# Chunked attention ahead of two gated products: from block 2 on two pairs of heads in one step, values and scores in one TensorE block, the first product on two PSUM banks

## Chip, core and metric

The kernel runs on one core of a Trainium2 chip. The metric is the device time of one execution in microseconds (us), the median of several executions.

## The reference

```python
# q, k, v: (4, 8, 768, 64); 8 memory keys and values for each head
for c in range(S // 32):
    l_start, r_end = max(0, 32 * c - 16), min(S, 32 * c + 32 + 8)
    k_full = concat(mem_k, k[:, :, l_start:r_end]); v_full = concat(mem_v, v[:, :, l_start:r_end])
    a = softmax(q[:, :, 32 * c:32 * c + 32] @ k_full.T / 8)      # sum + 1e-9 below the line
    out[:, :, 32 * c:32 * c + 32] = a @ v_full
x = out.transpose(0, 2, 1, 3).reshape(3072, 512)
h = x @ w1_in; x = (h * tanh(softplus(h))) @ w1_out              # 512 -> 2048 -> 512
h = x @ w2_in; return (h * sigmoid(1.702 * h)) @ w2_out          # 512 -> 2048 -> 512
```

The weights come in as 64-bit floats and are converted on the chip from their two 32-bit words.

## The kernel before

The 3072 tokens are 8 blocks of 384 (TB). A block has 8 heads; two heads that share the 128 partitions are a pair (hp, four of them), and 96 queries with a window of 128 keys are a group, four to a block. An *octet* is one pair of heads with all four groups of a block.

The work has four stages: the first product with the attention in between (`forward` and `quads`, 8 blocks x 16 tiles f of 128 outputs), the product of the first layer's output (`across`), the second layer's first product (`first`) and its second (`second`). From block 1 on, an operand of the first product is split into a high and a low part in a reduced 32-bit type, and a tile f is 4 x 3 = 12 matmuls of 384 columns into one PSUM bank (line 1049). Block 0 uses plain 32-bit matmuls and starts while weights are still being converted on VectorE (lines 377 to 394) and split for the later blocks (490 to 495).

The attention of an octet from block 1 on runs so: from block 2 on, q and k come by DMA in pieces of 32 x 32 and are turned by VectorE (lines 630, 634); `oct_scores` puts 16 matmuls into two banks (742); `quad`, for each half of the octet, takes the masked minimum on VectorE (794), the powers with their sums on ScalarE (809) and, after the inverses of the sums, the scaling on VectorE or ScalarE (829, 837); `oct_out` turns the weights on TensorE (938), copies them out (945, 947), multiplies with the values (959) and evicts the result as high and low part (973, 974, 978) into the next block's operands. Octets use the banks s0, s1 and o0, o1 in turn. A tile f goes in turn to two h banks and to o2 and o3, and is copied out by ScalarE or VectorE (1177, 1178), then sent to DRAM.

The order of instructions on every engine is made by a planner, `Plan`. Each operation is put in with a rank (the tile f at which it is due), a price for each engine that can do it, and what it reads and writes. `issue` runs through time: an engine that comes free takes the ready operation of the lowest rank. The resulting order is then issued; nothing changes it on the chip. The scores of an octet of block j have the rank 16 * (j - 1) - 12 + 4 * hp + 0.5, the tile f of block j has 16 * j + f. A buffer's name (`Tag`) has a number of places, and `Shared` puts buffers into parts of another: before the change q and k as loaded lie in one place each (in z0), as turned in one place each (in z1), and the turned weights in two (z3).

Weights of the later products are converted during the first one, in the order of a list (`layer, p`) with one entry for every 7 tiles f; for layer 1 and p below 4 the result stays in the buffers wo4 to wo15, wo0 and wo1.

Of the kernel before, what the change touches and what calls it, by code (L numbers as in the profile page):

```python
# [23 lines left out]
CUT = 6  # L24
STAGGER = 1.5

# [63 lines left out]

class Part:
# [17 lines left out]
class Plan:  # L109
# [4 lines left out]
    RELOAD = 1.4  # L114
    PATIENCE = 1.0
# [4 lines left out]
    def add(self, rank, ways, reads=(), writes=(), updates=(), chain=None, table=None):  # L120
        op = Op()
        op.table = table
        op.rank, op.ways, op.seq = rank, ways, len(self.ops)
# [9 lines left out]
        for b in (*writes, *updates):  # L133
            for o in b.readers:
                wait(o)
            b = b.whole
            if not b.users and b.tag is not None:
                made = b.tag.made
                k = made.index(b)
                if k >= b.tag.bufs:  # L140
                    b.gate += [(o, True) for o in made[k - b.tag.bufs].users]
                    made[k - b.tag.bufs].closed = True
                if k:
                    b.gate.append((made[k - 1].users[0], False))
# [25 lines left out]
    def issue(self):  # L170
# [14 lines left out]
        while left:  # L185
# [5 lines left out]
            for e in engines:  # L191
# [44 lines left out]
                lag = self.LAG.get(e, 0.0)  # L236
                if size:
# [27 lines left out]
def bus(nbytes, run):  # L265
    return nbytes / 270e3 * (1 if run >= 512 else 1.5 if run >= 256 else 2.5)
# [3 lines left out]
def kernel(  # L270
# [46 lines left out]
    def tags(pool, **bufs):  # L317
# [4 lines left out]
        z0=1, z1=1, z2=1, z3=1, vt=2, e=2, mx=3, sm=3, r=3, mask=1,  # L322
# [410 lines left out]
    def oct_scores(pair, rank, names):  # L733

        s = [T[n].new([GQ, GB, P], F32) for n in names]

        def scores():
            for queries, keys, _ in pair:
                for i in range(2):
                    for hh in range(2):  # L740
                        d = slice(hh * D, (hh + 1) * D)
                        nc.tensor.matmul(  # L742
                            out=s[hh][:, keys(d, i, True), :], lhsT=queries(d, i), rhs=keys(d, i), start=True, stop=True
                        )

        add(rank + 0.5, [("pe", 1.4, scores)], reads=list(dict.fromkeys(pair[0][2] + pair[1][2])), writes=s)
        return s
# [12 lines left out]
    def quad(j, hp, gp, heads, rank, given=None, both=None):  # L760
# [8 lines left out]
        e = T["ev" if j == 0 and hp % 2 else "e"].new([GQ, 2, 2, P], F32)  # L769
# [35 lines left out]
        for hh in range(2):  # L805
            add(rank + 0.6, [("dve", 0.42, lambda hh=hh: least(hh))], reads=[s[hh], mask], writes=[e, mx])
# [11 lines left out]
        for i in range(2):  # L818
            for hh in range(2):
                add(  # L820
                    rank + 1, [("act", 0.6, lambda i=i, hh=hh: power(i, hh))],
# [106 lines left out]
    def oct_out(j, hp, vt, rank, names, es):  # L928

        aTs = []  # L930
        for n, e in enumerate(es):
            t = T[names[n]].new([P, 2, 2, GQ], F32)
            aT = T["aT"].new([P, 2, 2, GQ], F32)

            def turn(t=t, e=e):
                for i in range(2):
                    for hh in range(2):
                        nc.tensor.transpose(t[:, i, hh, :], e[:, i, hh, :], ident[:GQ, :GQ])

            r = rank + STAGGER * n  # L940
            add(r + 2.2, [("pe", 0.33, turn)], reads=[e, ident], writes=[t])
            add(
                r + 2.4,
                [
                    ("act", act(TB, True), lambda t=t, aT=aT: nc.scalar.activation(
                        out=aT.get(), in_=t.get(), func=AF.Copy)),
                    ("dve", dve(TB), lambda t=t, aT=aT: nc.vector.tensor_copy(out=aT.get(), in_=t.get())),
                ],
                reads=[t], writes=[aT],
            )  # L950
            aTs.append(aT)
        o = T[names[1]].new([P, GB, GQ], F32)
        h = 2 * hp if j < EARLY else 2 * hp % HV
        per = GB // len(vt)

        def values():
            for g in range(GB):
                for hh in range(2):
                    nc.tensor.matmul(  # L959
                        out=o[hh * D:(hh + 1) * D, g], lhsT=vt[g // per][:, g % per, h + hh], rhs=aTs[g // 2][:, g % 2, hh],  # L960
                        start=True, stop=True,
                    )

        add(r + 2.7, [("pe", 1.0, values)], reads=[*vt, *aTs], writes=[o])
        if j not in x0:
            x0[j] = Inputs("xh", j), Inputs("xl", j)
        xh, xl = x0[j]
        part = fixed()
        flat = lambda: o.get().rearrange("p g t -> p (g t)")
        add(  # L970
            r + 2.9,
            [
                ("act", act(TB, True), lambda: nc.scalar.activation(out=xh.at(hp), in_=flat(), func=AF.Copy)),
                ("dve", dve(TB), lambda: nc.vector.tensor_copy(out=xh.at(hp), in_=flat())),
            ],
            reads=[o], writes=[xh.buf(hp), part],
        )
        add(r + 3.1, [("dve", dve(TB), lambda: nc.vector.tensor_tensor(
            out=xl.at(hp), in0=flat(), in1=xh.at(hp), op=ALU.subtract))], reads=[o, part], writes=[xl.buf(hp)])

    def quads():

        last = None
        for j in range(NB):
            b, s0 = divmod(j * TB, S)
# [3 lines left out]
            for n in range(NQ):  # L989
# [6 lines left out]
                else:  # L996
                    hp, gp = divmod(n, GB // 2)
                    if gp == 0:
# [5 lines left out]
                        else:  # L1004
                            pair = pair_of_heads(j, hp, rank)
# [544 lines left out]
```

## Time and profile before

| | us |
|---|---|
| median of 3 runs | 1124.51 (1123.49 to 1124.64) |
| profiled execution | 1122.46 |
| its span, first to last instruction | 1120.70 |
| busy: TensorE (PE) | 1103.0 (98%) |
| busy: VectorE (DVE) | 846.5 (76%) |
| busy: ScalarE (ACT) | 604.4 (54%) |

The profiled execution's own time holds what lies around the span. Matmuls are pipelined, so that a busy PE says that no matmul was missing, not that it ran at its peak. PEld is the weight load, which lies beside the matmuls. SP issues the DMAs.

### The profile page before, as it was taken

To read this page: it belongs to the slowest core of one execution; us is meant where nothing else is said; L and a number is where in the kernel's file an instruction comes from. 1 tells how busy PE (TensorE), PEld (TensorE's weight loads), DVE (VectorE), ACT (ScalarE), POOL (GpSimd) and SP (SyncE) were. 2 spreads that over 40 slices of the span, in tenths; PEclk is the share of its full clock that TensorE was granted. 3 is DMA by queue.
4 is the path that set the end of the run, shared out by engine and by line. 5 is a ranking of instruction groups with operands and counts; after the bars stand their busy time and mean duration, and the time that the engine had idled before them with its cause. 6 is when DMAs were issued, how large, how long until landed. Compare 5 with 4: busy or idle time off the path is not lost.

```text
span 1120.7 us, 22456 instructions
## 1 busy us (share of the span) xinstructions
PE 1103.0 (98%) x8226; PEld 1060.7 (95%) x8226; DVE 846.5 (76%) x1865; ACT 604.4 (54%) x1401; POOL 14.7 (1%) x35
## 2 busy tenths in 40 slices
PE   7899999999999999999999999999999999999998
PEld 6567999999999999999999999999999999999998
DVE  5899777987677578898888965747466786877875
ACT  4876555756466456645655565646565543333332
POOL 2000000000000000000000000000000000000000
PEclk9999999999999999999999999999999999999999
DMA  9975878768877946635742676867687735445351
GB/s 171 286 205 129 217 227 232 198 168 223 234 219 247 306 154 214 223 122 174 235 135 76 209 244 221 293 230 248 225 276 245 216 105 155 128 116 157 104 158 50
DMA packets 298222, 217.95 MB, mean 194 GB/s; under 512 B 136120, under 2 KB 276423, under 8 KB 298111
## 3 DMA queue, kind: packets, MB, share of 16 engines
q1 hardware_dynamic: 297759, 215.76, 65.3%
q8 instruction: 65, 1.06, 0.4%
q0 software_dynamic: 352, 0.75, 0.4%
q14 instruction: 46, 0.38, 0.1%
HBM read 135.18 MB, written 81.26 MB: 193 GB/s over the span
## 4 chain that ended last, share of the span: by engine, by line
PE 94%; DMA 2%; SPq 1%; DVE 1%; ACT 1%; issue 0%; DVEq 0%; ACTq 0%
PE h L1049 13%; PE o L1049 13%; PE o L1400 9%; PE o L1308 9%; PE h L1207 9%; PE o L1207 7%; PE h L1400 6%; PE s L1308 6%; PE h L1308 6%; PE s L1400 6%; PE s L1207 4%; PE o L742 1%; SPq L336 1%; PE s L742 1%; PE o L959 1%; PE s L959 1%
## 5 line engine op out<-in xcount | busy, mean ns | idle before, releaser
L809 ACT ACTIVATE e<-e,mx 96x128 f32<-96x128 f32 x240 | 93.0, 392 | 7.3 <-DVE mx L794 7.2
L1049 PE MATMUL o<-xh,wi 128*128 128x384 f32 x320 | 83.6, 342 | 0.0
L1049 PE MATMUL h<-xh,wi 128*128 128x384 f32 x320 | 83.2, 340 | 0.0
L1049 PEld LDWEIGHTS o<-xh,wi 128*128 128x128 f32 x320 | 56.7, 188 | 1.5
L1049 PEld LDWEIGHTS h<-xh,wi 128*128 128x128 f32 x320 | 57.0, 188 | 1.1
L1049 PE MATMUL h<-xl,wi 128*128 128x384 f32 x160 | 53.8, 336 | 0.0
L1049 PE MATMUL o<-xl,wi 128*128 128x384 f32 x160 | 53.7, 336 | 0.0
L1177 ACT ACTIVATE e<-h 128x384 f32<-128x384 f32 (+2 forms) x48 | 22.8, 475 | 45.6 <-PE h L1400 29.6
L809 ACT ACTIVATION_READ_ACCUMULATOR e<-e,mx 96x1 f32 x240 | 45.8, 191 | 0.0
L794 DVE CUSTOM_DVE_ANT_0 e<-s,mask 96x128 f32<-96x128 f32 x128 | 29.0, 281 | 20.9 <-PE s L778 8.3
L1400 PE MATMUL o<-wo,xh 128*128 128x256 f32 x232 | 43.9, 282 | 0.0
L1390 DVE TENSOR_TENSOR xl<-wi,xh 128x1024 fp32r<-128x1024 f32 x32 | 38.8, 1222 | 3.4 <-ACT xh L1387 2.6
L1308 PE MATMUL o<-xh,wo 128*128 128x256 f32 x224 | 40.5, 282 | 0.0
L794 DVE CUSTOM_DVE_ANT_0 e<-o,mask 96x128 f32<-96x128 f32 x112 | 25.1, 282 | 19.0 <-PE o L742 12.5
L1390 DVE TENSOR_TENSOR xl<-vt,xh 128x1024 fp32r<-128x1024 f32 x24 | 29.3, 1222 | 12.9 <-ACT xh L1387 12.2
L1291 DVE TENSOR_TENSOR xl<-z,xh 128x1024 fp32r<-128x1024 f32 x24 | 29.3, 1223 | 11.4 <-ACT xh L1287 10.7
L1387 ACT ACTIVATE xh<-wi 128x1024 fp32r<-128x1024 f32 x25 | 26.4, 1056 | 19.8 <-PE h L1400 10.0
L1049 PE MATMUL h<-wo,wi 128*128 128x384 f32 x192 | 36.7, 340 | 0.0
L1400 PEld LDWEIGHTS o<-wo,xh 128*128 128x128 f32 x232 | 35.9, 190 | 0.0
L1049 PE MATMUL o<-wo,wi 128*128 128x384 f32 x192 | 35.2, 337 | 0.0
L1308 PEld LDWEIGHTS o<-xh,wo 128*128 128x128 f32 x224 | 34.7, 190 | 0.0
L1049 PEld LDWEIGHTS h<-wo,wi 128*128 128x128 f32 x192 | 33.2, 188 | 0.7
(414 smaller groups left out, 3425.4 us busy)
## 6 DMA issues: line engine op xcount, KB each, us to landing
st<-in_moe_w_out_dram SPq DMA_DIRECT2D x32, 512.0 KB
st<-wd SPq DMA_DIRECT2D x29, 512.0 KB
g1d<-z SPq DMA_DIRECT2D x64, 192.0 KB
g1d<-gl SPq DMA_DIRECT2D x64, 192.0 KB
z<-g1d SPq DMA_DIRECT2D x24, 512.0 KB
vt<-gd SPq DMA_DIRECT2D x24, 512.0 KB
wi<-gd SPq DMA_DIRECT2D x24, 512.0 KB
wi<-in_moe_w_in_dram SPq DMA_DIRECT2D x16, 512.0 KB
```

What stands on the lines that cost most here:

```text
L742: nc.tensor.matmul(out=s[hh][:, keys(d, i, True), :], lhsT=queries(d, i), rhs=keys(d, i), start=True, stop=True)
L794: nc.vector.tensor_tensor_reduce(out=e[:, i, hh, :], in0=s[hh][:, first + i, :], in1=mask[:GQ, mask_of(g0 + i), :], scale=-scale, scalar=-NEG,
L809: nc.scalar.activation(out=e[:, i, hh, :], in_=e[:, i, hh, :], func=AF.Exp, scale=-1.0, bias=mx[:, i, hh:hh + 1], accum_out=sm[:, first + ...
L959: nc.tensor.matmul(out=o[hh * D:(hh + 1) * D, g], lhsT=vt[g // per][:, g % per, h + hh], rhs=aTs[g // 2][:, g % 2, hh], start=True, stop=True,
L1049: nc.tensor.matmul(out=h.get(), lhsT=a[:, c], rhs=b.at(kk), start=(n == 0), stop=(n == KD * len(prods) - 1))
L1177: ("act", act(n, True), lambda: nc.scalar.activation(out=dst(), in_=bank.get(), func=AF.Copy)),
L1207: nc.tensor.matmul(out=bank.get(), lhsT=a, rhs=b, start=(fresh and m == 0), stop=(m == 3 * K2 - 1), skip_group_check=not fresh,)
L1291: add(rank + 0.05, [("dve", dve(n2), lambda gh=gh, gl=gl, src=src: nc.vector.tensor_tensor(out=flat(gl), in0=flat(src), in1=flat(gh), op=A ...
L1308: nc.tensor.matmul(out=bank[:, d, :], lhsT=a, rhs=b[:, p, :], start=(fresh and h == d == p == m == 0), stop=(h == 1 and p == HP - 1 and m ...
L1387: ("act", act(NP * P), lambda: nc.scalar.activation(out=flat(gh), in_=flat(src), func=AF.Copy)),
L1390: add(rank + 0.05, [("dve", dve(NP * P), lambda: nc.vector.tensor_tensor(out=flat(gl), in0=flat(src), in1=flat(gh), op=ALU.subtract))], re ...
L1400: nc.tensor.matmul(out=bank.get(), lhsT=a[:, p], rhs=b, start=(fresh and p == 0 and m == 0), stop=(p == NP - 1 and m == 2), skip_group_che ...
```

## The change

From block 2 on, two octets (two pairs of heads) are handled as one step: their scores are one TensorE operation, and the values of the step before are put into the same operation ahead of them. The second octet's later operations have a rank 3 units higher (LATE). The second step of a block uses the bank pairs s0, o2 and o0, o3, so that the first product no longer has o2 and o3 from block 1 on; it uses the two h banks, is put in as two halves of 6 matmuls, and its copy has a rank 4 units lower (URGENT). q and k get two places, their turned form four, the turned attention weights four, in wo11 to wo15 (`Spread`). The conversion of the layer-1 output weights 2 and 3, which need those buffers, moves to the end of its list. The planner's prices for ScalarE and VectorE are lowered by 0.1 and 0.085 us below rank 110, with as much more delay until a result can be used, and the bus is taken as faster.

```diff
+URGENT = 4
+LATE = 3
+class Spread:
+    def __init__(self, before, *places):
+        self.before, self.places, self.bufs = before, places, len(places)
+        self.made = []
+
+    def new(self, shape, dtype):
+        b = Buf(self, shape, dtype)
+        b.inside, b.at = self.places[len(self.made) % self.bufs]
+        self.made.append(b)
+        return b
...
+    OVERLAP = {"act": 0.1, "dve": 0.085}
+    CALM = 110
...
+        lap = self.OVERLAP if rank < self.CALM else {}
+        op.ways = [(w[0], max(w[1] - lap.get(w[0], 0.0), 0.06), *w[2:]) for w in ways]
...
+                if op.rank < self.CALM:
+                    lag += self.OVERLAP.get(e, 0.0)
...
-    return nbytes / 270e3 * (1 if run >= 512 else 1.5 if run >= 256 else 2.5)
+    return nbytes / 290e3 * (1 if run >= 512 else 1.3 if run >= 256 else 1.8)
...
-        z0=1, z1=1, z2=1, z3=1, vt=2, e=2, mx=3, sm=3, r=3, mask=1,
+        z0=1, z1=1, z2=1, z3=1, vt=2, e=2, mx=5, sm=4, r=4, mask=1,
...
-    def oct_scores(pair, rank, names):
+    def oct_scores(pairs, rank, names, before=None):
+        if before:
+            values, r, given, made_by, evict = before
+            reads, writes, cost = reads + given, made_by, cost + 1.0 + 0.75 - 0.2
+            rank = min(rank, r - 0.5)
...
         def scores():
+            if before:
+                values()
+            for pair, s in zip(pairs, out):
...
+        if before:
+            evict()
+        return out
...
-        e = T["ev" if j == 0 and hp % 2 else "e"].new([GQ, 2, 2, P], F32)
+        e = T["ev" if j != 1 and hp % 2 else "e"].new([GQ, 2, 2, P], F32)
...
-    def oct_out(j, hp, vt, rank, names, es):
+    def oct_out(j, rank, vt, heads):
+        kept = []
+        for hp, names, es, late in heads:
...
+                r = rank + late + STAGGER * n
...
+        if j >= EARLY and (j, heads[-1][0]) != (NB - 1, H // 2 - 1):
+            return values, r + 2.7, reads, writes, evict
+        add(r + 2.7, [("pe", 1.0 + 0.75 * (len(kept) - 1), values)], reads=reads, writes=writes)
+        evict()
...
+            if j == EARLY:
+                more = [T[x].new([P, 2 * DM], F32) for x in ("wo15", "wo11", "wo12", "wo13", "wo14")]
...
+                T["ql"] = Spread(pre, (z0, 0), (more[3], 0))
+                T["kl"] = Spread(pre, (z0, TB), (more[3], TB))
+                T["qT"] = Spread(pre, *((z, 0) for z in (z1, *more[:3])))
+                T["kT"] = Spread(pre, *((z, 448) for z in (z1, *more[:3])))
+                T["aT"] = Spread(pre, (z3, 0), (z3, TB), (more[4], 0), (more[4], TB))
...
-                            pair = pair_of_heads(j, hp, rank)
+                            pair = pair_of_heads(j, hp, rank - 4 * (hp % 2))
...
+                        todo.append((hp, pair))
+                        many = 1 if j < EARLY else 2
+                        if len(todo) == many:
+                            r0 = rank - 4 * (many - 1)
...
+                            before = oct_out(j, r0, vals, heads)
+                            todo = []
...
-        h = T[("h", "h", "o2", "o3")[f % 4]].new([P, TB], F32)
+        h = T[("h", "h", "o2", "o3")[f % 4] if j == 0 else "h"].new([P, TB], F32)
...
+        grain = KD // 2 if j else KD
+        for k0 in range(0, KD, grain):
+            kks = range(k0, k0 + grain)
+            done = [pace[i]] if k0 + grain == KD else []
+            add(
+                i, [("pe", grain * (3 * 0.174 if j else 0.644), lambda kks=kks: go(kks))],
+                reads=[*xs, *ws1], writes=[*done, h],
+            )
...
-        copy(i + 0.3, View(t), h)
+        copy(i + 0.3 - (URGENT if j else 0), View(t), h)
...
-                layer, p = ((1, 4), (1, 5), (1, 6), (1, 7), (1, 0), (1, 1), (1, 2), (2, 0), (2, 1), (2, 2), (2, 3), (1, 3), (2, 4), (2, 5))[n]
+                layer, p = ((1, 4), (1, 5), (1, 6), (1, 7), (1, 0), (1, 1), (2, 0), (2, 1), (2, 2), (2, 3), (2, 4), (2, 5), (1, 2), (1, 3))[n]
```

## Rows read from the trace of the kernel before

**Rows 1.** Windows by stage: busy us of each engine (instructions), granted clock, DMA share.
```profile
core 0: us, PE busy (x) PEld busy (x) DVE busy (x) ACT busy (x) POOL busy (x), PEclk, DMA share, GB/s
0.00:40.00 40.00, 29.68 (x272) 24.48 (x272) 26.96 (x140) 24.02 (x99) 5.99 (x14) 0.93 1.02 203
40.00:97.40 57.40, 55.52 (x309) 34.98 (x306) 51.97 (x165) 41.82 (x130) 0.91 (x3) 0.99 0.78 211
97.40:397.80 300.40, 300.40 (x2276) 286.04 (x2275) 224.13 (x832) 177.40 (x602) 7.81 (x18) 1.00 0.79 223
```
**Rows 2.** TensorE's waits: who waited for whom, us in total, times, longest.
```profile
PE h L717 <- DMA wi<-in_q_dram: 3.8, 3, 2.9
...
PE o L1049 <- DVE wo L394: 1.3, 1, 1.3
```
**Rows 3.** Chain of work in the attention stage: start us, us, engine, tile, line, matmuls.
```profile
76.55 1.05 PE s L742 x16
...
101.13 2.30 PE h L1049 x12
...
191.17 0.66 PE o L938 x8
...
193.94 0.81 PE o L959 x16
194.75 1.05 PE s L742 x16
...
202.25 1.05 PE o L742 x16
...
214.62 0.81 PE o L938 x8
...
224.86 0.33 PE s L938 x4
225.19 2.11 PE h L1049 x12
227.30 0.33 PE s L938 x4
227.63 2.15 PE o L1049 x12
...
343.59 1.05 PE o L742 x16
...
358.87 0.81 PE o L959 x16
359.69 4.40 PE o L1049 x24
364.08 4.16 PE h L1049 x24
```
**Rows 4.** Timeline of single instructions around copies of the first product: start us, us.
```profile
205.26 0.34 PE L1049 MATMUL h<-xl,wi 128*128 128x384 f32 x1
...
207.39 0.39 ACT L809 ACTIVATE e<-e,mx 96x128 f32<-96x128 f32 x1
...
213.60 0.54 DVE L1178 COPY gl<-h 128x384 f32<-128x384 f32 x1
...
237.78 0.34 PE L1049 MATMUL h<-xl,wi 128*128 128x384 f32 x1
...
238.21 0.49 ACT L1177 ACTIVATE gl<-h 128x384 f32<-128x384 f32 x1 [0.89 <-ACT z L1177]
```
**Rows 5.** VectorE's groups, 97.4 to 397.8 us: count, busy us, mean ns, idle before.
```profile
L794 DVE CUSTOM_DVE_ANT_0 e<-o,mask 96x128 f32<-96x128 f32 x96 | 21.5, 282 | 19.0 <-PE o L742 12.5 <-PE s L938 6.5
L829 DVE TENSOR_TENSOR e<-e,r 96x512 f32<-96x512 f32 x32 | 21.0, 680 | 0.3
...
L634 DVE STREAM_TRANSPOSE z<-z 128x128 f32<-128x128 f32 x84 | 19.5, 278 | 0.0
...
L630 DVE STREAM_TRANSPOSE z<-z 128x384 f32<-128x384 f32 x21 | 11.9, 567 | 2.0 <-PE o L742 1.5 <-PE s L742 0.5
```

More of the change, by code (lines that the diff above doesn't have):

```diff
@@ L137, in add @@
             if not b.users and b.tag is not None:
+                if b.inside is not None and b.inside.tag.made[0] is not b.inside:
+                    below = b.inside.tag.made
+                    k = below.index(b.inside)
+                    b.gate += [(o, True) for o in below[k - 1].users]
+                    below[k - 1].closed = True
                 made = b.tag.made
                 k = made.index(b)
+                if isinstance(b.tag, Spread) and k < b.tag.bufs:
+                    b.gate += [(o, True) for o in b.tag.before.get(b.inside, ())]
                 if k >= b.tag.bufs:
@@ L731, in turned @@
         )
-    def oct_scores(pair, rank, names):
-        s = [T[n].new([GQ, GB, P], F32) for n in names]
-        def scores():
[L738 to L747, printed above, removed]
+    def oct_scores(pairs, rank, names, before=None):
+        reads, writes = [x for pair in pairs for p in pair for x in p[2]], []
+        cost = 1.4 + 1.0 * (len(pairs) - 1)
+        if before:
+            values, r, given, made_by, evict = before
+            reads, writes, cost = reads + given, made_by, cost + 1.0 + 0.75 - 0.2
+            rank = min(rank, r - 0.5)
+        out = [[T[n].new([GQ, GB, P], F32) for n in ns] for ns in names]
+        def scores():
+            if before:
+                values()
+            for pair, s in zip(pairs, out):
+                for queries, keys, _ in pair:
+                    for i in range(2):
+                        for hh in range(2):
+                            d = slice(hh * D, (hh + 1) * D)
+                            nc.tensor.matmul(
+                                out=s[hh][:, keys(d, i, True), :],
+                                lhsT=queries(d, i), rhs=keys(d, i), start=True, stop=True,
+                            )
+        add(
+            rank + 0.5, [("pe", cost, scores)],
+            reads=list(dict.fromkeys(reads)), writes=writes + [x for s in out for x in s],
+        )
+        if before:
+            evict()
+        return out
     def inverses(rank, sm, r):
@@ L805, in quad @@
         for hh in range(2):
-            add(rank + 0.6, [("dve", 0.42, lambda hh=hh: least(hh))], reads=[s[hh], mask], writes=[e, mx])
+            add(rank + 0.6, [("dve", 0.5 if rank + 0.6 < plan.CALM else 0.42, lambda hh=hh: least(hh))], reads=[s[hh], mask], writes=[e, mx])
         def power(i, hh):
@@ L820, in quad @@
                 add(
-                    rank + 1, [("act", 0.6, lambda i=i, hh=hh: power(i, hh))],
+                    rank + 1, [("act", 0.49 if rank + 1 < plan.CALM else 0.6, lambda i=i, hh=hh: power(i, hh))],
                     reads=[e, mx], writes=[done, sm], table="exp",
@@ L954, in oct_out @@
         per = GB // len(vt)
         def values():
[L957 to L979, printed above, removed]
+            for hp, aTs, o in kept:
+                h = 2 * hp if j < EARLY else 2 * hp % HV
+                for g in range(GB):
+                    for hh in range(2):
+                        nc.tensor.matmul(
+                            out=o[hh * D:(hh + 1) * D, g], lhsT=vt[g // per][:, g % per, h + hh],
+                            rhs=aTs[g // 2][:, g % 2, hh], start=True, stop=True,
+                        )
```

106 lines of the change are left out of this document (67 added, 39 removed).

## The prediction

> **What bounds the kernel now.** I read the busy time by stage first [rows 1]. From 97.4 to 397.8 us TensorE is busy for all 300.40 us, at a granted clock of 1.00. Before 97.4 us it lacks 10.3 us up to 40 and 1.9 us after it, while DMA runs at a share of 1.02 and then VectorE is busy for 51.97 of 57.40 us. So in the stage that the change is about (products of blocks 1 to 7 with attention between them) a gain can only come out of what TensorE spends itself; and before 97.4 us out of waits. The list of TensorE's waits [rows 2] says which: 3.8 us for the first loads of q, and 1.3 us for VectorE's conversion of a weight. The later stages are not touched by the change but for their order, and I give them no term.
>
> Then the chain of work, which in this stage is TensorE's own order, so that each row's time is what the row really cost [rows 3]. Two products of 12 matmuls behind another one take 4.16 us (364.08), so one takes 2.08. Behind transposes (L938) it takes 2.11, behind scores (L742) or values (L959) 2.30, and two there 4.40. So leaving scores or values for the product costs 0.22 to 0.24, I take 0.22; leaving transposes costs 0.03. The stretch from 97.4 to 397.8 us has 30 such leavings, from the row at 101.13 to that at 359.69. Scores straight behind values cost 1.05, as they do behind a product: the join values to scores is free. Transposes straight behind scores cost 0.81 in place of 0.66; 5 runs do. An octet (one pair of heads in one block) has one scores block and one values block; 22 scores blocks and 24 values blocks lie in the stretch.
>
> **What the change removes.** From block 2 on, two pairs of heads share one score block, and the values of a step stand in one block with the scores of the next. The work stays: 22 x 1.05 and 24 x 0.81 are paid as before. The number of leavings falls from 30 to 12 in this stretch (11 joined blocks, and the last values alone). That is 18 x 0.22 = 4.0 us. The 5 transposes behind scores go too, 5 x 0.15 = 0.75 us. Together 4.7 us. The two octets before 97.4 us add at most one or two leavings; I leave them out.
>
> **What it adds on TensorE.** The product is cut into two halves of 1.04 us, so that attention can come in at the half. The two transposes of a head pair come 0.68 us apart when VectorE scales both halves one after the other (L829) [rows 5]. Behind an indivisible 2.08 us most of them meet and run as x8; behind 1.04 us fewer will. A split one is seen at 224.86 and 227.30 [rows 3]: 0.33 each, with products of 2.11 and 2.15 behind them, so 0.33 + 0.03 + 0.33 + 0.07 against 0.66 + 0.03: 0.07 more (0.11 if the 0.04 excess of the product ahead of it is counted). The stretch has 22 pairs of transposes and 2 are split now. Between 0 and 20 more, 0 to 2.2 us. Two that come 0.68 apart fall on both sides of a border that recurs every 1.04 us in 0.68 / 1.04 of cases, two in three: 14 of 22, 12 more than now, at 0.07: 0.8 us.
>
> **Two banks in place of four.** Products of blocks 1 to 7 now alternate between the two h banks, 2.08 us each. With its engine free a copy starts 0.43 us after the last matmul starts (237.78 to 238.21) and ends 0.92 after it; bank h is wanted 2.25 us after it (0.17 to the next start, 2.08 for the other product). Such a copy leaves 1.33 us. But today copies come late: the product whose last matmul starts at 205.26 is copied at 213.60, 8.3 us later [rows 4], and nothing waits, because four banks cover it. That cover goes. In its place the change ranks the copy 4 units earlier (URGENT), so that it should be next on ScalarE or VectorE. Ahead of it then stands one running instruction, 0.68 us for L829 [rows 5]. The lower bound is nothing. The upper one: if one product in ten came 0.68 late, 11 x 0.68 = 7.5 us. I take 0.4 us, near the lower end, because 1.33 us is twice that instruction.
>
> What is queued behind the urgent copies is attention's own work on VectorE and ScalarE (busy 224 and 177 of 300 us [rows 1]), and TensorE's values wait for that. The allowance is wide: from the first scores of block 2 at 76.55 to the first product of block 7 at 364.08 are 287.5 us for 12 steps, 24 us a step [rows 3].
>
> **Edits costed at nothing.** The planner's prices (OVERLAP, the shorter powers, a faster bus) change only orders. Extra q, k and transposed buffers lie in weight slots that are idle in this stage; their loads come earlier, on SP's queue, while DMA has a share of 0.79. Block 2's second head pair now asks for its q and k at the first one's rank, so eight more DMA issues stand ahead of weight loads on SP's queue: rival 4 prices it. Converting weights (1,2) and (1,3) later puts VectorE work into the last products. VectorE as a whole is busy 75% of the stage; if it were not done by 397.8, the next stage's first product would wait, which I put at 0 to 2 us.
>
> **The sum.** The profiled execution took 1122.46 us, 1.76 of it around its span of 1120.70. 4.7 - 0.8 - 0.4 = 3.5 us less: 1119.0 for an execution like it. The median of the runs is 1124.51, 2.05 above that execution; against it I predict **1121.0 us**. The likeliest case by itself lies from 1118.5 to 1122.2.
>
> **Rivals.**
> 1. *Nothing is left* (chance 0.20). The joined block does not have the free inside that single rows show, or all 22 transposes split. If values to scores cost inside the block what leaving costs, 11 x 0.22 = 2.4 us go back: 1123.4. If all transposes split at 0.11, 2.2 - 0.8 = 1.4 us go back: 1122.4. With both, 1124.8. For it: that a block inside may hide a cost in the 1.05. Against it: 1.05 at 194.75 behind values and at 202.25 behind a product [rows 3]. (The Trainium skill, TensorEngine Tiling (Array Packing), section Tiling Modes under Key Properties, says that changing the tiling mode drains the engine. Values use column halves and scores row halves, so by that rule the join should cost a drain as well, and the sum would be 1123.4. The trace agrees for the way back to the full array, 0.22, and not for the join, where no excess shows.)
> 2. *Slower through two banks* (0.12). Copies come behind plan, TensorE waits at each. It decides from 4.7 - 0.8 = 3.9 us on, 0.035 us for each of 112 products; at 0.68 us for one in seven, 16 x 0.68 = 10.9 against 3.9: 1131.5. At one in ten, 7.5 against 3.9, 1128.1.
> 3. *Slower through lockstep* (0.05). Both head pairs start together, so their powers queue: scores to values of one octet took 343.59 to 358.87, 15.3 us [rows 3]; eight more powers at 0.39 [rows 4] are 3.1 us, and eight more mask minima at 0.28 are 2.2 [rows 5]. 20.6 against 24 us. Only from 24 us on is a block late; at 25 us, 12 us are lost, and 3.5 stand against them: 1133.
> 4. *The first 97 us move* (0.15, of it 0.12 to the better, 0.03 to the worse). An octet's VectorE work is 0.57 + 4 x 0.28 for the turns, 8 x 0.28 for the minima, 2 x 0.68 for the scaling, 5.3 us [rows 5]. Put ahead of the weight conversions in a stage where VectorE is busy for 91% it could hold back the first block's products by 5.3 less the 2.5 us (1.05 + 0.66 + 0.81) that TensorE spends on that octet: 2.8 us, 1123.8 with the gain still there; on two octets, 1126.6. The other way, prices nearer to what instructions occupy (a power 0.39 where the plan had 0.6) may take a third of the 12.2 us that TensorE lacks up to 97.4: 4 us, 1117.0.
>
> My forecast has the remaining 0.48. A difference under 0.2%, 2.25 us, is what a measurement here cannot tell from none. Faster holds the forecast and the better part of rival 4, 0.60; the same is rival 1 and the worse part of rival 4, 0.23; slower is rivals 2 and 3, 0.17. The range goes from 1115.5, just below the better case, to 1127.5, past rival 1 and the worse part of rival 4, and almost to the lighter case of rival 2; what lies beyond is about 0.14 above and 0.05 below.
>
> **What would show it.** In the changed kernel's chain, L959 x32 followed by L742 x32 with 1.6 and 2.1 us, a product of 2.3 (or a half of 1.26) behind it, about 12 such blocks, and fewer than 15 leavings at 0.22; the stretch from the first block-1 product to the first L1308 falls by about 4 us. Waits of TensorE for L1177 or L1178 would show rival 2, a wait of the product for L974 or L978 rival 3, an earlier or later first product of block 1 rival 4. The prediction is wrong if values to scores shows an excess, if waits of the product for its bank add up to more than 2 us, or if the first 97 us change by more than 2 us.

## The result, and the profile after

The changed kernel takes 1133.02 us (median of 5, 1132.64 to 1135.78) against 1124.51 us, a ratio of 1.0086 [1.0071, 1.0101]: 8.5 us slower, and outside the predicted range, on the other side of no change. Its profiled execution took 1132.64 us, its span is 1130.3 us, 9.6 longer than before.

The windows of the changed kernel, first the stages of [rows 1], then the stage from its first product of block 1 to the first matmul of the second stage, and four microseconds inside it (columns as there):

```profile
0.00:40.00 40.00, 30.05 (x275) 24.83 (x276) 25.83 (x135) 25.45 (x102) 5.99 (x14) 0.87 1.01 203
40.00:97.40 57.40, 56.23 (x316) 35.87 (x315) 53.90 (x182) 41.19 (x128) 5.19 (x4) 1.00 0.87 226
97.40:397.80 300.40, 287.94 (x2216) 275.65 (x2215) 222.37 (x826) 173.41 (x585) 3.43 (x11) 0.99 0.77 215
95.00:406.00 311.00, 298.54 (x2278) 286.16 (x2275) 229.22 (x856) 177.63 (x602) 3.43 (x11) 0.99 0.76 214
192.00:196.00 4.00, 4.00 (x40) 3.44 (x38) 0.81 (x2) 0.92 (x2) 0.00 (x0) 0.57 1.03 277
```

The third row stands against 300.40 of 300.40 in [rows 1]: TensorE now lacks 12.5 us in a stage where it lacked nothing. The first product of block 1 starts at 95.0, 3.0 us earlier than the 98.0 of before, and the second stage at 406.0 in place of 397.6. So the stage is 311.0 us long against 299.6, and 311.0 - 298.5 = 12.5 of it are idle. TensorE's own work in it is 298.5 against 299.6 us: 1.1 us less, where the forecast had 3.9 less for leavings and transposes. The low granted clock of the fifth row takes back up to 4.00 x 0.43 = 1.7 us of that. The later stages are 1.2 us longer. -3.0 + 11.4 + 1.2 is the 9.6 of the span.

TensorE's waits in the changed kernel from 95 to 406 us say what it lacked (columns as in [rows 2]):

```profile
PE o L983 <- DVE ev L872: 5.1, 4, 3.0
PE s L983 <- DVE e L872: 2.2, 2, 1.1
PE h L1130 <- ACT z L1262: 1.6, 1, 1.6
PE h L1130 <- ACT gl L1262: 1.2, 1, 1.2
PE h L1130 <- DVE gl L1263: 1.1, 1, 1.1
PE s L983 <- ACT e L880: 0.5, 1, 0.5
PE o L983 <- DVE e L872: 0.4, 1, 0.4
```

L983 is the transpose of the weights (938 before), L872 and L880 the scaling (829, 837), L1130 the product, L1262 and L1263 its copies (1177, 1178). The transposes wait 5.1 + 2.2 + 0.4 = 7.7 us for VectorE's scaling, and the product 1.6 + 1.2 + 1.1 = 3.9 us for its bank. Another 0.5 us of the transposes' waits is for ScalarE's scaling, 8.2 us in all. This sum is the larger one, and no rival spoke of it.

What VectorE waits for, from 90 to 400 us, in the changed kernel:

```profile
DVE u L467 <- DMA wd<-u: 20.7, 8, 5.5
DVE v L467 <- DMA wd<-v: 11.7, 4, 4.6
...
DVE wo L662 <- DMA wo<-in_k_dram: 4.1, 2, 2.3
...
DVE wo L658 <- DMA z<-in_q_dram: 3.2, 1, 3.2
```

and in the kernel before, the one wait of that kind:

```profile
DVE u L439 <- DMA wd<-u: 0.2, 1, 0.2
```

L467 (439 before) combines two converted weight quarters in place, after the old content has been written out to DRAM (wd); L658 and L662 (630, 634) turn loaded q and k. Waiting for transfers in those lines rose from 0.2 to 39.7 us. How one of them reaches TensorE stands in the timeline of the changed kernel:

```profile
188.26 0.43 DVE L467 TENSOR_TENSOR v<-v 128x256 f32<-128x256 f32 x1 [4.04 <-DMA wd<-v]
...
190.02 1.28 DVE L872 TENSOR_TENSOR ev<-ev,r 96x512 f32<-96x512 f32 x2
...
190.75 1.15 PE L983 MATMUL o<-ident,ev 96*128 96x96 f32 x8 [2.99 <-DVE ev L872]
```

VectorE stands 4.04 us in front of a combine, the inverses and the scaling come behind it, and TensorE, whose order is fixed too, stands 2.99 us in front of the transposes. What holds up a write-out is seen on SP's queue before the longest wait:

```profile
260.25 2.81 SPq L364 DMA_DIRECT2D z<-in_q_dram  x3
...
263.66 1.98 SPq L364 DMA_DIRECT2D wo<-in_k_dram  x4
...
266.26 0.38 SPq L364 DMA_DIRECT2D wd<-v  x1
266.73 0.40 SPq L364 DMA_DIRECT2D wd<-u  x1
...
268.83 0.42 DVE L467 TENSOR_TENSOR u<-u 128x256 f32<-128x256 f32 x1 [5.49 <-DMA wd<-u]
```

Loads of q and k stand ahead of the write-outs and take 2.81 us (one of the three 1.82) and 1.98 us of issuing. VectorE stood from 263.34 on: 3.39 us until the write-out of u began to be issued, most of it behind the four loads of k, and 2.10 more until its data were out. From there the wait runs on through ScalarE to a bank:

```profile
269.50 0.40 ACT L852 ACTIVATE e<-e,mx 96x128 f32<-96x128 f32 x1 [2.83 <-DVE mx L837]
...
269.90 0.47 ACT L1262 ACTIVATE z<-h 128x384 f32<-128x384 f32 x1
...
270.42 0.62 PE L1130 MATMUL h<-xh,wi 128*128 128x384 f32 x2 [1.65 <-ACT z L1262]
```

The minima (L837) come late from VectorE, ScalarE stands 2.83 us in front of a power, the copy that frees the bank comes behind it, and the product waits 1.65 us. So the bank waits of this kernel are no measure of the two banks alone: all three come within 6 us behind a wait of VectorE for a write-out (4.57, 5.49 and 4.69 us). Of TensorE's waits over 0.2 us in the stage, 12.1 us, such a wait of VectorE for a transfer stands within 6 us ahead of 10.6 us; the 6 us behind all such waits fill a third of the stage.

The joined blocks came as worked out. A joined block in the chain of the changed kernel, and the last values (L779 scores, L1005 values):

```profile
258.93 1.47 PE o L1005 x32
260.40 1.05 PE s L779 x16
261.45 0.87 PE o L779 x16
262.32 2.30 PE h L1130 x12
...
345.89 1.47 PE o L1005 x32
```

Values of two octets take 1.47 us, their scores 1.92 straight behind, and the product behind the block takes 2.30 as in [rows 3]. The second 16 scores take 0.87 where the first take 1.05: the first pay 0.18 for coming behind values.

### The profile page after: what moved, and what is told of

It reads as the page before. It is cut to its first block, busy times and chain, and to the rows that moved or that the text cites. A ratio compares the mean times of both kernels' runs of the same rounds, so it can differ in the third digit from the quotient of the medians.

```text
span 1130.3 us, 22386 instructions
## 1 busy us (share of the span) xinstructions
PE 1101.3 (97%) x8226; PEld 1060.7 (94%) x8226; DVE 855.3 (76%) x1887; ACT 593.9 (53%) x1375; POOL 14.6 (1%) x29
## 3 DMA queue, kind: packets, MB, share of 16 engines
q8 instruction: 64, 1.05, 0.4%
## 4 chain that ended last, share of the span: by engine, by line
PE 79%; DVE 8%; DMA 6%; SPq 4%; issue 2%; ACT 1%; DVEq 0%; ACTq 0%
PE h L1130 14%; PE o L1485 9%; PE o L1393 9%; PE h L1292 8%; PE o L1292 7%; PE h L1485 6%; PE h L1393 6%; PE s L1485 6%; PE s L1393 6%; SPq L364 4%; PE s L1292 4%; DMA vt<-in_v_dram 2%; DMA wi<-in_moe_w_in_dram 1%; PE o L1005 1%; PE s L779 1%
## 5 line engine op out<-in xcount | busy, mean ns | idle before, releaser
L1130 PE MATMUL h<-xh,wi 128*128 128x384 f32 x640 | 165.7, 340 | 2.7 <-ACT z L1262 1.6
L1130 PEld LDWEIGHTS h<-xh,wi 128*128 128x128 f32 x640 | 114.0, 188 | 4.6 <-ACT z L1262 2.0
L1130 PE MATMUL h<-xl,wi 128*128 128x384 f32 x320 | 107.5, 336 | 0.0
L1130 PE MATMUL h<-wo,wi 128*128 128x384 f32 x384 | 70.9, 339 | 1.2 <-ACT gl L1262 1.2
L1130 PEld LDWEIGHTS h<-wo,wi 128*128 128x128 f32 x384 | 66.1, 188 | 2.1 <-ACT gl L1262 1.5
L852 ACT ACTIVATE e<-e,mx 96x128 f32<-96x128 f32 x144 | 55.9, 392 | 10.8 <-DVE mx L837 10.6
L1130 PEld LDWEIGHTS h<-xl,wi 128*128 128x128 f32 x320 | 60.2, 188 | 0.0
L1262 ACT ACTIVATE z<-h 128x384 f32<-128x384 f32 x47 | 22.9, 487 | 56.9 <-PE h L1130 48.5
L1262 ACT ACTIVATE e<-h 128x384 f32<-128x384 f32 (+2 forms) x47 | 22.4, 477 | 47.3 <-PE h L1485 28.8
L852 ACT ACTIVATE ev<-ev,mx 96x128 f32<-96x128 f32 x112 | 43.4, 390 | 0.0
L1475 DVE TENSOR_TENSOR xl<-wi,xh 128x1024 fp32r<-128x1024 f32 x32 | 38.8, 1223 | 5.3 <-ACT xh L1472 4.1
L1262 ACT ACTIVATE gl<-h 128x384 f32<-128x384 f32 x45 | 21.9, 486 | 38.6 <-PE h L1130 30.0
L837 DVE CUSTOM_DVE_ANT_0 e<-s,mask 96x128 f32<-96x128 f32 x104 | 24.5, 281 | 16.9 <-PE s L821 11.5
L1485 PE MATMUL o<-wo,xl 128*128 128x256 f32 x116 | 32.8, 283 | 0.0
L1393 PE MATMUL o<-xl,wo 128*128 128x256 f32 x112 | 31.6, 283 | 0.0
```

The costliest lines, as they stand in the source:

```text
L837: nc.vector.tensor_tensor_reduce(out=e[:, i, hh, :], in0=s[hh][:, first + i, :], in1=mask[:GQ, mask_of(g0 + i), :], scale=-scale, scalar=-NEG,
L852: nc.scalar.activation(out=e[:, i, hh, :], in_=e[:, i, hh, :], func=AF.Exp, scale=-1.0, bias=mx[:, i, hh:hh + 1], accum_out=sm[:, first + ...
L1130: nc.tensor.matmul(out=h.get(), lhsT=a[:, c], rhs=b.at(kk), start=(n == 0), stop=(n == KD * len(prods) - 1))
L1262: ("act", act(n, True), lambda: nc.scalar.activation(out=dst(), in_=bank.get(), func=AF.Copy)),
L1393: nc.tensor.matmul(out=bank[:, d, :], lhsT=a, rhs=b[:, p, :], start=(fresh and h == d == p == m == 0), stop=(h == 1 and p == HP - 1 and m ...
L1475: add(rank + 0.05, [("dve", dve(NP * P), lambda: nc.vector.tensor_tensor(out=flat(gl), in0=flat(src), in1=flat(gh), op=ALU.subtract))], re ...
```

## The experiments

All kernels here do the whole work. "Start" is the first product of block 1, "stage" the time from it to the first matmul of the second stage, "idle" what TensorE lacks in it; all from the profiled executions, us. In e6, c1 and g1 the stage holds one tile of block 0, 2.8 us.

| kernel | ratio to before [95%] | start | stage | idle |
|---|---|---|---|---|
| before | 1 | 98.0 | 299.6 | 0.0 |
| changed | 1.0086 [1.0071, 1.0101] | 95.0 | 311.0 | 12.5 |
| e1_old_bus | 1.0069 [1.0050, 1.0088] | 97.8 | 303.2 | 7.9 |
| e2_old_prices | 1.0047 [1.0030, 1.0064] | 99.4 | 302.5 | 6.9 |
| e3_before_new_prices | 1.0064 [1.0047, 1.0082] | 94.7 | 309.3 | 8.0 |
| e4_late_wd | 1.0161 [1.0133, 1.0189] | 96.3 | 314.3 | 13.1 |
| e5_two_banks | 1.0050 [1.0031, 1.0070] | 98.4 | 304.3 | 2.3 |
| e6_bus_only | 1.0148 [1.0127, 1.0169] | 101.2 | 310.9 | 6.2 |
| e7_wd_pool | 1.0005 [0.9983, 1.0027] | 94.3 | 301.6 | 5.5 |
| e8_four_banks | 1.0048 [1.0024, 1.0072] | 98.1 | 305.3 | 7.6 |
| e9_old_prices_wd_pool | 1.0102 [1.0083, 1.0121] | 100.1 | 302.7 | 6.6 |
| c1_before_nudge | 1.0036 [1.0026, 1.0046] | 98.4 | 302.4 | 0.0 |
| g1_before_nudge_up | 1.0035 [1.0024, 1.0046] | 97.6 | 302.6 | 0.0 |
| c2_after_nudge | 1.0085 [1.0060, 1.0110] | 97.0 | 307.5 | 9.4 |
| g2_wd_pool_nudge | 1.0019 [1.0002, 1.0035] | 94.9 | 299.7 | 5.5 |
| g3_before_wd_pool | 1.0066 [1.0051, 1.0081] | 99.3 | 301.3 | 0.6 |
| e11_best | 1.0017 [1.0005, 1.0029] | 97.1 | 296.0 | 2.2 |
| f1_bus_late | 0.9945 [0.9931, 0.9960] | 94.5 | 295.8 | 2.0 |
| f3_no_pool | 0.9963 [0.9949, 0.9978] | 94.3 | 295.5 | 2.2 |
| f4_nudge | 1.0042 [1.0027, 1.0057] | 96.0 | 301.3 | 5.3 |

### Prices or structure

The theory was that the planner's new prices put VectorE's work ahead of the transfers that it needs; the rival, that the structure (two banks, four turned places) does it. e1 takes the bus price back, e2 all prices, e3 puts the new prices on the kernel before. e4 plans the write-outs later, to see whether the combines as such are to blame.

```diff
# e1
-    return nbytes / 290e3 * (1 if run >= 512 else 1.3 if run >= 256 else 1.8)
+    return nbytes / 270e3 * (1 if run >= 512 else 1.5 if run >= 256 else 2.5)
# e2: e1 and
-    OVERLAP = {"act": 0.1, "dve": 0.085}
+    OVERLAP = {}
...
# powers 0.6, minima 0.42 at every rank
# e3: the kernel before with OVERLAP, CALM, the 290e3 bus, powers 0.49, minima 0.5
# e4: the changed kernel, write-outs into wd
-            load(rank, done[-1], [...], P * 4 * n, 4 * n, [t])
+            load(rank, done[-1], [...], P * 4 * n, 4 * n, [t], late=4.0)
```

> The changed kernel, with the planner's bus price as it was (270 kB per us, 1.5 and 2.5 for short runs). Theory A, transfers priced too low: the combinations at L467 no longer wait 32 us for the weight write-out, the transposes hardly wait for the scaling, and TensorE's idle time between the first block-1 product and L1393 falls from 12.5 us to under 4 us: 1120 to 1125 us. Theory B, the structure (two h banks, two pairs of heads in lockstep): the waits stay, 1130 us or more. Theory C, the engine prices (OVERLAP, shorter powers): they stay too, 1129 us or more.

> The changed kernel with all prices as they were: bus, no OVERLAP, powers 0.6 and minima 0.42. Theories A and C: TensorE idles under 2 us in the stage, and what joining saves shows: 1119 to 1124 us, by C clearly below the run with the old bus alone, by A the same within 2 us. Theory B: 1130 us or more.

> The kernel before with the new prices alone (bus, OVERLAP, powers 0.49, minima 0.5), four banks and single octets. Theories A and C: waits of VectorE for write-outs and of TensorE appear here too, 1127 to 1134 us. Theory B: as before or better, 1121 to 1125 us.

> The changed kernel; the planner takes the write-outs of converted weights (wd) as landing 4 us later, so that the combinations that overwrite their source stand later in VectorE's order. Nothing else is priced otherwise. If those 32 us of waits on VectorE are what TensorE pays for: 1122 to 1127 us, with under 5 us of waits at L467. If they are a by-product of everything being late: 1130 to 1135 us, with waits at other VectorE instructions in their place.

e3 is the clearest: with nothing of the structure, the prices make the stage 9.7 us longer, 8.0 of them idle, all before the transposes. Its waits, TensorE's and then VectorE's (from 90 to 410 us; L944 the transposes, L835 and L843 the scaling, L445 the combines):

```profile
PE s L944 <- DVE e L835: 6.0, 3, 3.8
...
PE s L944 <- ACT e L843: 2.0, 1, 2.0
...
DVE u L445 <- DMA wd<-u: 15.7, 10, 3.3
...
DVE v L445 <- DMA wd<-v: 6.6, 4, 2.9
```

The same two lists as in the changed kernel. e1 shows which price it is. With the old bus price VectorE's combines wait 8.6 us in place of 32.4 (8.4 of them in the row below), and the transposes 1.7 in place of 8.2; none of TensorE's waits over 0.2 us comes within 6 us behind a wait for a transfer.

```profile
DVE u L467 <- DMA wd<-u: 8.4, 4, 3.0
```

But 7.9 us idle stay where the theory had under 4, and 5.9 of them are waits of the product for its banks, so that the time hardly falls. With all old prices (e2) the stage is 302.5, TensorE's own work in it 295.6, 4.0 us less than before; but 6.9 us idle are left, most of them at the product's banks (4.4 us, 3.1 of them in the first row) and at the values:

```profile
PE h L1130 <- DVE z L1263: 3.1, 4, 1.5
PE o L1005 <- DVE wo L992: 1.6, 1, 1.6
```

e2 met neither branch: it idles more than 2 us and is under 1130. So the structure has its gain and a cost of its own, and the prices a second cost; with all old prices the change is still 0.47% slower than the kernel before. e4 missed: the waits of the combines fell to 3.6 us, but those of the lines that turn q and k rose from 7.3 to 16, and the ratio rose from 1.0086 to 1.0161. Its waits of VectorE and TensorE:

```profile
DVE wo L662 <- DMA wo<-in_k_dram: 10.1, 4, 4.0
...
DVE u L467 <- DMA wd<-u: 1.8, 2, 1.1
...
PE o L983 <- DVE ev L872: 9.2, 6, 3.4
```

What costs is not the combines but any instruction that VectorE's fixed order puts ahead of its transfer.

### Banks, the bus alone, another queue

e5 is the kernel before with two h banks, halves and the urgent copy. e6 is the kernel before with the new bus price alone. e7 is the changed kernel with the write-outs on GpSimd's queue. e8 has e2's prices, four banks for the product and no joined blocks (two octets in s0, s1 and o0, o1).

```diff
# e5
-        h = T[("h", "h", "o2", "o3")[f % 4]].new([P, TB], F32)
+        h = T[("h", "h", "o2", "o3")[f % 4] if j == 0 else "h"].new([P, TB], F32)
...
+        grain = KD // 2 if j else KD
...
-        copy(i + 0.3, View(t), h)
+        copy(i + 0.3 - (URGENT if j else 0), View(t), h)
# e6: the kernel before
-    return nbytes / 270e3 * (1 if run >= 512 else 1.5 if run >= 256 else 2.5)
+    return nbytes / 290e3 * (1 if run >= 512 else 1.3 if run >= 256 else 1.8)
# e7: keep()'s load, ways[1:] is GpSimd's queue
+            add(rank, ways[1:] if pool else ways if early else ways[:1], reads=reads, writes=[buf])
# e8
-        h = T[("h", "h", "o2", "o3")[f % 4] if j == 0 else "h"].new([P, TB], F32)
+        h = T[("h", "h", "o2", "o3")[f % 4]].new([P, TB], F32)
```

> The kernel before with one part of the change: products of blocks 1 to 7 on the two h banks, cut into halves, their copies ranked 4 units earlier. Octets stay single, prices as they were. If two banks cost what the run with old prices shows (4.5 us of waits of the product for L1178-like copies out of 7): 1126 to 1130 us, with waits of the product of 3 to 6 us. If those waits come from two pairs in lockstep: under 1 us of them, 1121 to 1125 us.

> The kernel before with the cheaper bus alone. If the cheap bus is what lets VectorE wait for transfers and TensorE for the scaling: over 15 us of VectorE waits for transfers, 5 to 9 us of TensorE waits before the transposes, first block-1 product about 3 us earlier, 1126 to 1131 us. If the engine prices do that (OVERLAP, powers): under 5 us of such waits, 1120 to 1125 us.

> The changed kernel with the write-outs of converted weights issued by GpSimd's queue in place of SP's; prices as changed. If VectorE's waits come from these issues being late behind SP's loads: the waits at L467 fall from 32 us to under 8, TensorE's idle time in the stage from 12.5 to under 8 us, 1125 to 1130 us. If the transfers themselves are late (16 shared DMA engines) or every load is: the waits stay or move to q and k (L658, L662), 1131 to 1140 us.

> The changed kernel with old prices, four banks for the product, and so only s0, s1, o0, o1 for the two octets of a step and the values as an operation of their own (no join). If two banks are the larger loss of the structure: no waits of the product for its bank, 1121 to 1125 us, below the run with old prices alone (1128). If the lockstep is: scores and values now wait for one another's banks, attention falls behind and a block's first product waits for the evicted values, 1130 us or more.

e5 costs 4.7 us of stage: 2.3 idle, 2.1 of it at the bank (its wait below; L1050 the product), and the product's own time rises from 241.6 to 244.3, with halves left 59 times for attention where whole tiles were left 47 times.

```profile
PE h L1050 <- ACT z L1182: 2.1, 3, 1.0
```

e6 has a stage of 310.9 us, 6.2 of it idle, and VectorE's combines waiting 16.1 us for write-outs, with the bus price alone, on the old structure. TensorE's share of it does not lie where it was expected, 5 to 9 us before the transposes: there it waits 0.6 us, and 5.6 before scores.

```profile
DVE u L439 <- DMA wd<-u: 14.4, 8, 4.0
...
PE o L742 <- POOL z L640: 2.3, 2, 1.3
PE s L742 <- DVE xl L978: 2.1, 1, 2.1
PE s L742 <- POOL z L640: 1.2, 1, 1.2
```

L640 is a copy on GpSimd that waits for VectorE's turns of k, L978 an eviction. 3.9 of the 6.2 us come within 6 us behind a wait of VectorE for a write-out. And block 1 started 3.2 us later than before, not 3 earlier.

e7 is the counterpart: with the write-outs out of SP's queue VectorE's waits for them fall from 32.4 to 4.1 us, the idle time from 12.5 to 5.5, and the ratio from 1.0086 to 1.0005. What is left there is a k load and the transposes behind it:

```profile
DVE wo L662 <- DMA wo<-in_k_dram: 6.9, 2, 4.6
DVE u L467 <- DMA wd<-u: 4.1, 3, 2.1
...
PE o L983 <- DVE ev L872: 4.5, 2, 3.5
```

e8, which gives up the join for four banks, is no better than e2 (1.0048 and 1.0047): the product waits 0.5 us for banks, but the scores wait 5.3 for evictions out of theirs:

```profile
PE s L779 <- DVE xl L1028: 3.4, 3, 1.3
PE s L779 <- DVE wo L1028: 1.9, 2, 1.1
```

### How much any new order moves

Each price moves the whole written order. c1 and g1 make the bus of the kernel before 0.7% dearer or cheaper (268e3 and 272e3 for 270e3), c2 that of the changed kernel (288e3 for 290e3), g2 that of e7. g3 is the kernel before and e9 is e2, each with the write-outs on GpSimd's queue.

```diff
# c1; g1 has 272e3
-    return nbytes / 270e3 * (1 if run >= 512 else 1.5 if run >= 256 else 2.5)
+    return nbytes / 268e3 * (1 if run >= 512 else 1.5 if run >= 256 else 2.5)
# c2 on the changed kernel, g2 on e7
-    return nbytes / 290e3 * (1 if run >= 512 else 1.3 if run >= 256 else 1.8)
+    return nbytes / 288e3 * (1 if run >= 512 else 1.3 if run >= 256 else 1.8)
```

> The kernel before with a bus price dearer by 0.7% (268 in place of 270 kB per us), which says nothing new of the chip. Theory D, that any other order of the planner's moves the time by some us: 1127 to 1135 us, with TensorE waits of several us. Theory A (only prices that put work ahead of its transfers cost time): within 2 us of the kernel before.

> The changed kernel with a bus price dearer by 0.7% (288 in place of 290). Theory A: 1131 to 1135 us, waits of VectorE at L467 around 30 us as in the changed kernel. Theory D: anywhere from 1123 to 1142 us.

> The kernel before with a bus price cheaper by 0.7% (272 in place of 270). If its order is one that happens to fit: 1126 to 1130 us as with the nudge the other way. If that nudge was the exception: 1122 to 1125 us.

> The changed kernel with write-outs on GpSimd's queue and a bus price dearer by 0.7% (288 in place of 290). If SP's late issues are the cause of half the loss: 1121 to 1127 us, waits of VectorE for write-outs under 8 us, as in the run without the nudge (1123.8). If that run was luck: 1128 to 1135 us.

> The kernel before with write-outs on GpSimd's queue, nothing else. It has no waits for write-outs (0.2 us), so nothing is to be had there: 1123 to 1127 us, 4 us of it for a new order. If GpSimd's issues disturb VectorE or DMA: 1128 us or more.

> The changed kernel with old prices (1128.2 us) and the write-outs of weights on GpSimd's queue. If the late issue of SP is what is left of the loss there (VectorE waits of 5.7 us for the write-outs and 4.9 for stores, which make the product wait for its banks): TensorE idles under 3 us in the stage and the 4.1 us that joining saves show: 1120 to 1124 us. If two banks wait by themselves: 4 to 5 us of waits of the product remain, 1126 to 1129 us.

Both nudges of the kernel before cost 0.35%, 4 us, with no idle time in the stage: its 302.4 and 302.6 us are all TensorE work, 2.8 of them the tile of block 0. Without it the stage is as long as before. Of the 5.4 us by which c1's span is longer, 0.4 + 2.8 are block 0, which ends later, and 2.1 lie behind the stage. In c1 TensorE's granted clock is low for longer ahead of the stage, 0.85 over the first 45 us against 0.92 in the kernel before; the windows row of c1 around the place:

```profile
37.00:45.00 8.00, 6.97 (x41) 5.04 (x42) 7.02 (x23) 7.39 (x25) 0.00 (x0) 0.57 0.96 255
```

The clock is not all of it: at a mean granted clock of 0.997 c1 took 1125.0 and 1125.9 us, the kernel before beside it 1121.7 to 1122.3.

All three other orders of the old structure at old prices that ran (c1, g1, g3) lost 0.35% or more. So the order of the kernel before is a favourable one. But what c1 and g1 lost lies ahead of the stage and behind it, and g3 lost 1.7 us in it; the changed kernel lost 11.4 in the stage.

The idle time in the stage tells causes apart only in part: 0.0 to 0.6 us for all four orders of the old structure at old prices (before, c1, g1, g3), 8.0 and 6.2 with new prices on it (e3, e6), but 9.4 and 12.5 for two orders of the changed kernel, and 2.0 to 7.9 for seven orders of the new structure with joined blocks and the old bus price in blocks 1 to 7. What TensorE's waits stand behind tells more. Waits over 0.2 us in the stage that come within 6 us behind a wait of VectorE for a transfer:

| new bus price | us, of all | old bus price in blocks 1 to 7 | us, of all |
|---|---|---|---|
| changed | 10.6 of 12.1 | e1 | 0 of 7.5 |
| c2 | 9.2 of 9.2 | e2 | 3.7 of 6.8 |
| e3 | 7.9 of 7.9 | e9 | 0 of 6.3 |
| e4 | 10.8 of 12.2 | e11 | 0.3 of 1.5 |
| e6 | 3.9 of 6.2 | f1 | 0.2 of 1.4 |
| e7 | 4.5 of 5.3 | f3 | 1.2 of 2.1 |
| g2 | 4.2 of 5.3 | f4 | 0 of 4.9 |

So the waits behind late transfers belong in the main to the new bus price, on either structure (in e2 and f3 they are mostly for stores of the product). e1, e9 and f4 show that an order without them can idle 5 to 8 us for other reasons.

g3 and e9 missed their forecasts: the other queue is worth nothing by itself at the old prices, 1.0066, and 1.0102 against 1.0047. g3 lies in the branch that named a disturbance by GpSimd's issues, and no run tests that. e9's span is 7.6 us longer than e2's, 0.7 of it at the start, 0.2 in the stage and the rest in the stages behind it; that I did not follow.

### A version that beats both

e11 keeps the new engine prices only below rank 16 (CALM) and the new bus price only below rank 12, with e7's queue. f1 has the new bus price also from rank 128 on. f3 is f1 with the write-outs on SP again, f4 is f1 with both bus prices 0.7% dearer. So f3 differs from the changed kernel in prices alone.

```diff
# f1; e11 without the second half of the condition
-    CALM = 110
+    CALM = 16
...
+def bus(nbytes, run, rank):
+    if rank < 12 or rank >= 128:
+        return nbytes / 290e3 * (1 if run >= 512 else 1.3 if run >= 256 else 1.8)
+    return nbytes / 270e3 * (1 if run >= 512 else 1.5 if run >= 256 else 2.5)
```

> The changed kernel with new prices only for work due in block 0 (engines below rank 16, bus below rank 12), old ones after it, and write-outs on GpSimd's queue. If the new prices earn their 3 us in the first block and lose them later: first block-1 product at 94 to 96 us, TensorE idle under 4 us in the stage, 1118 to 1122 us. If the order of the first block decides how the stage starts and the gain is not separable: 1123 to 1128 us.

> The changed kernel with write-outs on GpSimd's queue, new engine prices below rank 16 only, and the old bus price only for work due between ranks 12 and 128 (blocks 1 to 7), the new one elsewhere. If the last stage of the run before it was lost by its own order (waits of 3.9 us, half clock after one of them): product stage 296 us as there, last stage 243 us in place of 248, 1118 to 1121 us. If the last stage comes out at random: 1119 to 1127 us.

> The version of 1116.8 us with the write-outs back on SP's queue. If the queue is what the change needs beside its prices: VectorE's waits for write-outs rise from 4.6 to over 10 us, TensorE idles 6 us or more in the product stage, 1121 to 1127 us. If the prices alone do it: 1115 to 1120 us.

> The version of 1116.8 us with both bus prices dearer by 0.7%. If its gain is the mechanism's (4 us of leavings, 3 us in the first block, few waits): 1115 to 1121 us. If it is one order among many: 1121 to 1128 us.

e11 has the short stage (296.0 us), but its later stages are 6.9 us longer than f1's, and it ends no faster than the kernel before. f1 takes 1116.80 us (1116.06 to 1118.25) against 1123.34 beside it: 6.5 us faster than before and some 16 faster than the change as it was. Its windows:

```profile
0.00:94.50 94.50, 83.26 (x577) 58.04 (x577) 76.67 (x293) 63.84 (x214) 7.61 (x18) 0.96 0.93 218
94.50:390.30 295.80, 293.77 (x2275) 284.75 (x2274) 238.27 (x872) 172.45 (x601) 25.00 (x53) 1.00 0.80 225
```

Both gains are there: the start 3.5 us earlier, the stage 3.8 shorter with 2.0 idle. f3 keeps most of it without the other queue: the changed kernel goes from 1.0086 to 0.9963 by prices alone. f4 loses some 11 us by the nudge, 5.5 of them in the stage: f1 is a good order among others, picked by running it, and not a property of its prices.

## Why the prediction was wrong

**"The planner's prices (OVERLAP, the shorter powers, a faster bus) change only orders."** This step failed. Orders were the whole cost. The step named VectorE's 75% as cover; but a busy share is no cover for an engine that takes its instructions in a fixed order. With the cheaper bus VectorE's combines and turns were written where their transfers were thought to have landed; 39.7 us of waiting for them (0.2 before) stand ahead of 10.6 of TensorE's 12.1 us of waits, most of them at the transposes. e3 shows it without the structure, e1 that these waits go with the bus price (8.2 us at the transposes became 1.7), and f3 that prices alone can turn the sign. But the step does not carry the miss by itself: with all old prices (e2) the change is still 0.47% slower, in an order with other waits. The same paragraph sent the q and k loads ahead "while DMA has a share of 0.79" and looked at the weight loads behind them, not at the write-outs; e7 shows that queue, and the SP rows above how for one wait.

**"I take 0.4 us, near the lower end"** for two banks in place of four. A mis-sized term in most orders: where next to no late transfer stands ahead of them, the product's waits for its bank are 5.9 us in e1 and 2.1 in e5, and they are 4.4 in e2, above the 2 us that the prediction gave as its own refutation. In f1 they are 0.2, in e9 1.8. So the term depends on the order as much as on the banks. The halves add 2.7 us to the product's time in e5, where the prediction put 0.8 for split transposes. Rival 2 had this mechanism; its lighter case (7.5 us against 3.9) is above all of these. e8 shows that four banks move the wait to the scores.

**What was right, and what was luck.** Leavings and transposes: 4.7 - 0.8 = 3.9 us predicted; TensorE's own work fell by 1.1 in the changed kernel, by 299.6 - 295.6 = 4.0 in e2 and by 299.6 - 293.8 = 5.8 in f1. That 4.0 meets 3.9 is luck. The prediction had scores and values "paid as before", and took all of the gain from the product and the transposes. From start to start in the stage, us:

| | before | e2 | f1 |
|---|---|---|---|
| product | 241.6 | 240.5 | 239.8 |
| scores and values | 42.6 | 39.0 | 38.8 |
| transposes | 15.3 | 15.8 | 15.1 |

Scores and values are left 12 times, as predicted, but the halves eat most of what that saves (and transposes are left 29 times against 18 in the changed kernel). The larger gain was not in the sum: the second half of a joined block is cheaper than its parts in [rows 3], 1.47 against 2 x 0.81 and 1.92 against 2 x 1.05.

The reading behind rival 1 was wrong, though the rival fell. "The join values to scores is free" compared 1.05 behind values with 1.05 behind a product, and both hold the price of a change: scores behind scores take 0.87. So the join costs 0.18 us, no more than the way in from the product, which the prediction had paid already. The Trainium skill (TensorEngine Tiling (Array Packing), Key Properties under Tiling Modes) says that changing the tiling mode drains the engine. The trace agrees at the join too (1.05 against 0.87), as on the way back to the full array (2.30 against 2.08).

**Rival 4's better part came too.** The first product of block 1 starts 3.0 us earlier (0.12 given, 4 us forecast), more than the 2 us that the prediction named as a sign of being wrong. With the new engine and bus prices together in block 0 the start lies between 94.3 and 97.1, without the one or the other or both between 97.6 and 101.2 (e1 97.8, e6 101.2, e2 99.4). **Rival 3 did not come**: the last values of attention run at 345.89, 13 us earlier than in [rows 3].

**What stays open.** The parts are not additive below some 4 us, because each is another order. The waits for transfers go with the bus price, but what the engine prices cost in blocks 1 to 7 of the new structure isn't settled: e1 has them and 7.9 us idle, e2 has not and 6.9, and one order of each is too few. Why the sum of e2's gain and loss comes out at +2.9 in the stage and f1's at -3.8, with like prices there, is known only as 6.9 against 2.0 us of waits and 295.6 against 293.8 of work, not from a rule of the planner.

## What to carry to other kernels

Where a planner writes the order, its prices are part of the change: cost them by asking which instruction would now stand ahead of a transfer on an engine that cannot pass it, and which queue that transfer's issue waits in. Before a cause is taken for found, nudge one price by under a percent on both kernels, and compare where the time is lost and what each wait of the bound engine stands behind, since the total and the idle time both move. Reusing a bank sooner can cost where copies come late now, even when no row of before shows a wait. And a price read from rows that all hold it, such as the way into a block, looks like nothing.

## What the runs showed of the hardware

A wait of TensorE cost more than itself. After the 2.99 us that ended at 190.75, the granted clock from 192 to 196 us was 0.57, mostly the lower level of 1.2 GHz, and a joined block's values ran in 2.67 us there (1.48 and 1.19) in place of 1.47:

```profile
193.37 1.48 PE s L1005 x16
194.84 1.19 PE o L1005 x16
```

A like stretch begins at the end of the 3.8 us wait in e3, and others behind waits of 1.4 to 4.0 us in e4, c2 and f4; a wait of 2.7 us in g2 and one of 2.3 in e9 were not followed by one. The kernel before has none in this stage.

A change between the kinds of block costs TensorE 0.15 to 0.22 us, and the first block of a kind pays it: values take 0.81 and then 0.66 (1.47 for two), scores 1.05 and then 0.87, a product 2.30 and then 2.08. Behind transposes the product pays 0.03.

Issues stand in line on a queue: from 95 to 350 us of the changed kernel SP took 0.47 us for a load of q or k and 0.38 for a write-out at the median, and 1.9 at most, and the four loads of k took 1.98 of the 3.39 us above.
